# A second MLP product with wide matmuls, a third buffer of weight parts, and a fixed VectorE order

## The chip, the cores and the metric

The kernel runs on one core of a Trainium2 chip. The metric is the device time of one execution in microseconds. Five engines work side by side, each through its own list of instructions in order: TensorE (PE in the profile, with its weight loads as PEld), VectorE (DVE), ScalarE (ACT), GpSimd (POOL) and SyncE (SP), whose queue issues most of the transfers. They wait for one another through semaphores.

## The reference

One transformer-like block on x of 2048 tokens by 512 channels, in float32:

```
h  = x + linear_attention(layernorm(x))            # hedgehog feature map, 32 heads of 16
z  = layernorm(h)                                  # (2048, 512)
u  = gelu(z^T @ w1 + b1)                           # over the token axis: (512, 1792)
y  = u @ w2 + b2                                   # (512, 2048)
out = h + y^T
```

Only the last product, `u @ w2` with its bias and the addition to h, concerns the change. It makes an output of 2048 by 512 from 1792 hidden units. Three quarters of the kernel (attention, second layernorm, first MLP product) come before it and stay as they are.

## The kernel before

Products are made at close to float32 accuracy out of a format that TensorE takes at full pace: each operand is split into a high part (rounded, made by ScalarE as a copy) and a low part (the rest, made by VectorE as a subtraction), and a product is three matmuls: high by high, high by low, low by high. The function `mm3` (lines 61 to 65) does so in the earlier stages, always with 512 columns.

The second MLP product (lines 722 to 859) uses a Winograd-like scheme on blocks of two by two: for two row tiles of the output and two halves of its columns it needs seven block products where a plain product needs eight. The terms used below:

- A *pair* is two output tiles of 128 tokens (`sp`, eight of them). A *step* is one pair `sp` with one pair of hidden tiles `p` (seven of them), so there are 56 steps. A step makes seven block products, each of three matmuls 128 by 128 by 256 (L801): the left operand is one of seven combinations of w2's blocks, the right one of seven combinations of the hidden units' blocks with its high and low part side by side (`UB[p, m]`, 2 by 256 columns).
- A *group* is two steps (`GRP`). `stream_w2` (L779) prepares the seven combinations of w2 for one group: two transfers into `wraw` (L785), four additions and subtractions on VectorE (L789 to L792, here the *block sums*), the high part `whi` on ScalarE and the low part `wlo` on VectorE (the function `split`, L58 and L59; each over 1792 columns). `wraw` has three buffers, `whi` and `wlo` two each. The block sums read and write all of a `wraw`, so ScalarE's copy of that group comes after them.
- The seven products of a pair add up, over its seven steps, in four PSUM banks of 2 by 256 columns. Pairs take the four banks of pool `ps_b` and the four of `ps_f` and `ps_q` in turn. When a pair is done, ScalarE copies one half bank (`e`, L832) and VectorE makes the two output tiles from the banks (L833 to L837, here the *pair sums*: three additions of 256 columns and two fused additions of 512). GpSimd's queue adds each tile to h in memory (L839).
- The last pair works differently: its rows of h are loaded early (`hb`, L844) and the last three steps' products are run bank after bank, so that VectorE can finish the banks while others are still in work.

Around this part the program is ordered by a scheduler that lays out each engine's instructions from modelled times. It may move VectorE's block sums, low parts and pair sums past one another, and matmuls of high parts ahead of those of low parts. In the built program, VectorE's block sums run one group ahead: the list reads low part of group g, block sums of group g+2, low part of group g+1, block sums of group g+3, and so on, with the pair sums put between single block sums of one group.

Of the kernel before, what the change touches and what calls it, by code (L numbers as in the profile page):

```python
# [9 lines left out]
F32 = mybir.dt.float32  # L10
F32R = mybir.dt.float32r
AF = mybir.ActivationFunctionType
ALU = mybir.AluOpType
# [4 lines left out]
P = 128  # L18
S, D, H, DH, F = 2048, 512, 32, 16, 1792
NT = S // P  # L20
# [14 lines left out]
def block_kernel(ctx: ExitStack, tc: tile.TileContext, x, xT, wT, phic, wo, w1, b1, w2, b2,  # L35
                 kvmask, ident_in, out):
    nc = tc.nc
# [9 lines left out]
    b2s = cst.tile([P, NT], F32, name="b2s")  # L47
# [8 lines left out]
    def split(hi, lo, src, lo_engine):  # L56

        nc.scalar.activation(hi, src, AF.Copy)  # L58
        lo_engine.tensor_sub(lo, src, hi)  # L59

    def mm3(o, ah, al, bh, bl, first, last):

        nc.tensor.matmul(o, ah, bh, start=first, stop=False)  # L63
        nc.tensor.matmul(o, ah, bl, start=False, stop=False)  # L64
        nc.tensor.matmul(o, al, bh, start=False, stop=last)  # L65


    aq = ExitStack()
    ps_q = ctx.enter_context(tc.tile_pool(name="ps_q", bufs=2, space=PSUM, side="right"))
# [5 lines left out]
    sums = wqp.tile([P, SUMS, NPR, 2, 2], F32, name="smq")  # L75
# [284 lines left out]
    q = {"mm": 0, "logits": 0, "exp": 0, "sum": 0}  # L360
# [39 lines left out]
    for t in range(3, NT - 1):  # L400
        if t + 2 < NT:
            raw = load_x(t + 2)
# [108 lines left out]
    ps_f = ctx.enter_context(tc.tile_pool(name="ps_f", bufs=2, space=PSUM, reuse_waits="tile"))  # L511
# [83 lines left out]
    w2v = w2.rearrange("(k p) s -> p k s", p=P)  # L595
# [9 lines left out]
    def flush(n=None):  # L605
        if n is None:
            his()
        for _ in range(len(LATER) if n is None else min(n, len(LATER))):
            wl_, raw, wh_ = LATER.pop(0)
            LO.append(nc.vector.tensor_sub(wl_, raw, wh_).ins)  # L610
# [7 lines left out]
        COMING.append((wl_, raw, wh_))  # L618
        return wh_, wl_

    PU, WI, LO = {}, {}, []
    FN, FL = [0] * (NF // 2), [0] * (NF // 2)

    def fill_load(p):
        if FL[p] < NT:
            WI[p, FL[p]] = stream(w1v, FL[p], 2, p * 256, 256)
            FL[p] += 2

    def fill(p, pool=None):

        t = FN[p]
        FN[p] = t + 1
        if FL[p] <= t:
            fill_load(p)
            flush()
        if t == 0:
            PU[p] = [pool.tile([P, D], F32, name="pu", tag="pu") for _ in range(2)]
        a, b = WI[p, t - t % 2]
        for c in range(2):
            mm3(PU[p][c], a[:, t % 2, c * P:(c + 1) * P], b[:, t % 2, c * P:(c + 1) * P],  # L640
                HN[t][:, 0], HN[t][:, 1], t == 0, t == NT - 1)

    def q_half(i):
# [89 lines left out]
    U, UB, far = {}, {}, {}  # L733
# [43 lines left out]
    AW = {}  # L777

    def stream_w2(n):  # L779
        steps = STEPS[n:n + GRP]  # L780
        raw = ws.tile([P, GRP, 7, P], F32, name="wraw", bufs=3)
        wh_ = ws.tile([P, GRP, 7, P], F32R, name="whi")
        wl_ = ws.tile([P, GRP, 7, P], F32R, name="wlo")
        for i, (sp, p) in enumerate(steps):
            nc.sync.dma_start(raw[:, i, 0:4].rearrange("p (k i) s -> p k (i s)", k=2),  # L785
                              w2v[:, 2 * p:2 * p + 2, sp * 2 * P:(sp + 1) * 2 * P])
            AW[sp, p] = wh_[:, i], wl_[:, i]
        with tc.issue_after(LO[-18]):
            nc.vector.tensor_add(raw[:, :, 4], raw[:, :, 0], raw[:, :, 2])  # L789
            nc.vector.tensor_sub(raw[:, :, 0], raw[:, :, 1], raw[:, :, 0])  # L790
            nc.vector.tensor_sub(raw[:, :, 5], raw[:, :, 4], raw[:, :, 1])
            nc.vector.tensor_sub(raw[:, :, 6], raw[:, :, 3], raw[:, :, 5])  # L792
        split(wh_, wl_, raw, nc.vector)


    PROD = ((1, 1, 0, 0, True), (2, 6, 2, 1, True), (3, 3, 3, 1, True), (4, 4, 2, 0, False), (0, 0, 1, 0, True),
            (5, 5, 0, 1, False), (6, 2, 3, 0, False))

    def product(o, a, b, start, stop):
        for i, (x, y) in enumerate(((0, 0), (0, 1), (1, 0))):  # L800
            nc.tensor.matmul(o, a[x], b[:, y], start=start and i == 0, stop=stop and i == 2, skip_group_check=True)  # L801

    def products(sp, ps, order):
        for a, b, bk, half, opens in order:
            for p in ps:
                wh_, wl_ = AW[sp, p]
                product(bank[bk][:, half], (wh_[:, a], wl_[:, a]), UB[p, b], p == 0 and opens, p == NP - 1)

    def flat(a):
        return a.rearrange("p k d -> p (k d)")  # L810

    for n, (sp, p) in enumerate(STEPS):
        t = 2 * sp
        last = t + 2 == NT
        if n % GRP == 0:
            stream_w2(n)
        if p == 0:
            pools = [ps_f, ps_f, ps_q, ps_q] if sp % 2 else [ps_b] * 4
            bank = [pool.tile([P, 2, HD], F32, name="py", tag="pu") for pool in pools]
        if p < NP - 1 - 2 * last:  # L820
            products(sp, [p], PROD)
            continue
        if p < NP - 1:
            continue
        by_bank = sorted(PROD, key=lambda m: m[2:4])
# [3 lines left out]
        if not last:  # L829
            products(sp, [p], by_bank)  # L830
            ot = uo.tile([P, 2, 2, HD], F32, name="ot", bufs=1)
            nc.scalar.activation(e[:, 1], bank[0][:, 0], AF.Copy)  # L832
            nc.vector.tensor_add(u2, bank[0][:, 1], e[:, 1])  # L833
            nc.vector.tensor_add(u3, bank[1][:, 0], u2)
            nc.vector.tensor_add(e[:, 0], bank[2][:, 0], u2)
            for i, add in enumerate((u3.unsqueeze(1).to_broadcast([P, 2, HD]), e)):
                nc.vector.scalar_tensor_tensor(ot[:, i], bank[2 + i], b2s[:, t + i:t + i + 1], add,  # L837
                                               op0=ALU.add, op1=ALU.add)
                nc.gpsimd.dma_start(out[(t + i) * P:(t + i + 1) * P, :], flat(ot[:, i]), accum_op=ALU.add)  # L839
            continue  # L840

        hb = [hp.tile([P, 2, HD], F32, name=f"hb{i}") for i in range(2)]
        for i in range(2):
            nc.sync.dma_start(flat(hb[i]), out[(t + i) * P:(t + i + 1) * P, :])  # L844
            nc.vector.tensor_scalar(hb[i], hb[i], b2s[:, t + i:t + i + 1], None, op0=ALU.add)
        products(sp, [p - 2, p - 1, p], by_bank)
        nc.scalar.activation(e[:, 1], bank[0][:, 0], AF.Copy)
        nc.vector.tensor_add(hb[1][:, 1], bank[0][:, 0], hb[1][:, 1])
        nc.vector.tensor_add(u2, bank[0][:, 1], e[:, 1])
        nc.vector.tensor_add(hb[1][:, 0], u2, hb[1][:, 0])  # L850
        nc.vector.tensor_add(u3, bank[1][:, 0], u2)
        nc.vector.tensor_add(hb[0], hb[0], u3.unsqueeze(1).to_broadcast([P, 2, HD]))
        nc.vector.tensor_add(hb[0][:, 0], bank[2][:, 0], hb[0][:, 0])
        nc.vector.tensor_add(hb[1][:, 0], bank[2][:, 0], hb[1][:, 0])
        nc.vector.tensor_add(hb[0][:, 1], bank[2][:, 1], hb[0][:, 1])
        nc.sync.dma_start(out[t * P:(t + 1) * P, :], flat(hb[0]))
        for k, q in ((0, nc.scalar), (1, nc.sync)):
            nc.vector.tensor_add(hb[1][:, k], bank[3][:, k], hb[1][:, k])
            q.dma_start(out[(t + 1) * P:NT * P, k * HD:(k + 1) * HD], hb[1][:, k])


def _layout(A_x, A_wqkv, A_w_phi, A_wo, B_w1, B_b1, B_w2, B_b2):
# [44 lines left out]
```

## Time and profile before

| | |
|---|---|
| median of 3 runs | 526.39 us (526.26 to 526.75) |
| the profiled execution | 526.04 us, of which the span of the instructions 524.3 us |
| TensorE busy | 517.7 us, 99% of the span |
| VectorE busy | 384.5 us, 73% |
| ScalarE busy | 277.8 us, 53% |
| second MLP product | from 378.6 us on; its last matmul starts at 519.61 us |

The profile's page has a chain of work that ended last, followed back from the end; groups of equal instructions with their busy time, the mean duration of one and what ended the idle time ahead of them; lists of waits; and a timeline in which each line has a start, a duration, the engine, the line of the program, what is written and read (`wlo<-wraw,whi`) and, in brackets, idle time before it with what ended it. The windows give each engine's busy time in a stretch, with a count of instructions. A few per cent of the matmul records are missing from a trace, so counts of matmuls come from the program.

### The profile page before, as it was taken

The numbers are of one execution on the slowest core, as the hardware profiler recorded it, in microseconds if no ns is written. First come the engines' busy times: TensorE is split into PE (matmuls) and PEld (weight loads), VectorE is DVE, ScalarE is ACT, GpSimd is POOL, SyncE is SP. The second block draws the span as 40 slices with busy tenths as digits, with TensorE's granted clock in tenths as the row PEclk, the third lists the DMA queues.
The fourth block names the chain that finished last, engine by engine and source line by source line (L and its number), as shares of the span: only waits on it lengthen the run. The fifth ranks groups of instructions, "written<-read, shape, count | busy, mean of one in ns | idle before, by whom it ended". The sixth has DMA issues, their size and how long they took to land.

```text
span 524.3 us, 10150 instructions
## 1 busy us (share of the span) xinstructions
PE 517.7 (99%) x4000; PEld 446.6 (85%) x4000; DVE 384.5 (73%) x681; ACT 277.8 (53%) x475; POOL 229.4 (44%) x174
## 2 busy tenths in 40 slices
PE   8999999999999999999999999999999999999996
PEld 7888888887877777777788888888899999999996
DVE  6893999986997899697336425726668878888774
ACT  6999853434267877767756433426544333343330
POOL 2579698985989999974224000000001101101110
PEclk9999999999999999999999999999999999999999
DMA  8643210021303333333255432532015556535631
GB/s 304 198 132 121 75 47 22 1 83 60 103 21 101 102 101 108 115 101 123 81 173 154 115 101 81 181 102 80 20 41 122 144 139 154 126 123 133 150 71 50
DMA packets 45487, 55.85 MB, mean 107 GB/s; under 512 B 3968, under 2 KB 33024, under 8 KB 45440
## 3 DMA queue, kind: packets, MB, share of 16 engines
q1 hardware_dynamic: 43136, 51.38, 30.9%
q0 software_dynamic: 2016, 3.67, 5.3%
q8 instruction: 31, 0.51, 0.4%
q10 hardware_dynamic: 288, 0.17, 0.1%
q14 instruction: 16, 0.13, 0.1%
HBM read 46.81 MB, written 8.39 MB: 105 GB/s over the span
## 4 chain that ended last, share of the span: by engine, by line
PE 95%; DVE 3%; ACT 1%; issue 0%; DVEq 0%; ACTq 0%
PE py L801 26%; PE pu L63 13%; PE pu L64 12%; PE pu L65 12%; PE pv L64 3%; PE pv L65 3%; PE po L63 3%; PE pv L63 3%; PE po L65 3%; PE po L64 3%; PE pk_ps L63 2%; PE pk_ps L65 2%; PE pk_ps L64 2%; PE pn L549 2%; PE tr L531 2%; PE kvp L208 2%
## 5 line engine op out<-in xcount | busy, mean ns | idle before, releaser
L839 POOL DMA_DIRECT2D out<-ot x14 | 12.4, 996 | 210.9 <-DVE ot L837 210.9
L801 PE MATMUL py<-uf,whi 128*128 128x256 f32 x560 | 96.2, 283 | 0.0
L58 ACT ACTIVATE whi<-wraw 128x1792 fp32r<-128x1792 f32 x28 | 47.7, 1704 | 77.9 <-PE py L801 73.8
L63 PE MATMUL pu<-hs,whi 128*128 128x512 f32 x224 | 87.7, 394 | 0.0
L64 PE MATMUL pu<-hs,whi 128*128 128x512 f32 x224 | 87.2, 389 | 0.0
L65 PE MATMUL pu<-hs,wlo 128*128 128x512 f32 x224 | 86.7, 389 | 0.0
L801 PEld LDWEIGHTS py<-uf,whi 128*128 128x128 f32 x560 | 83.3, 192 | 0.0
L610 DVE TENSOR_TENSOR wlo<-wraw,whi 128x512 fp32r<-128x512 f32 x56 | 47.3, 847 | 44.7 <-ACT whi L603 44.5
L59 DVE TENSOR_TENSOR wlo<-wraw,whi 128x1792 fp32r<-128x1792 f32 x28 | 56.6, 2022 | 18.6 <-ACT whi L58 18.6
L801 PE MATMUL py<-uf,wlo 128*128 128x256 f32 x280 | 69.9, 283 | 0.0
L603 ACT ACTIVATE whi<-wraw 128x512 fp32r<-128x512 f32 x56 | 34.6, 625 | 45.0 <-PE pu L64 40.8
L63 PEld LDWEIGHTS pu<-hs,whi 128*128 128x128 f32 x224 | 42.0, 188 | 9.1 <-ACT hj L581 0.2
L801 PEld LDWEIGHTS py<-uf,wlo 128*128 128x128 f32 x280 | 49.7, 192 | 0.0
L65 PEld LDWEIGHTS pu<-hs,wlo 128*128 128x128 f32 x224 | 42.0, 188 | 8.9
L64 PEld LDWEIGHTS pu<-hs,whi 128*128 128x128 f32 x224 | 42.1, 188 | 8.5
L443 POOL TENSOR_TENSOR ez<-eq,zB 128x1024 f32<-128x1024 f32 x16 | 38.5, 2408 | 4.4 <-ACT zB L487 4.4
L801 PE MATMUL py<-un,whi 128*128 128x256 f32 x224 | 38.4, 283 | 0.0
L196 POOL TENSOR_TENSOR pk<-pk,sk 128x1024 f32<-128x1024 f32 x16 | 31.0, 1941 | 7.7 <-DVE sk L195 5.4
L467 POOL TENSOR_TENSOR eq<-eq,w 128x1024 f32<-128x1024 f32 x16 | 32.4, 2025 | 3.2 <-DVE w L464 3.2
L801 PEld LDWEIGHTS py<-un,whi 128*128 128x128 f32 x224 | 33.2, 192 | 0.1
L200 POOL TENSOR_TENSOR zacc<-zacc,pk 128x1024 f32<-128x1024 f32 x13 | 31.2, 2404 | 0.5
L172 ACT ACTIVATE pk<-pk,r 128x1024 f32<-128x1024 f32 x16 | 18.4, 1147 | 17.9 <-DVE pk L150 17.7
(172 smaller groups left out, 1174.6 us busy)
## 6 DMA issues: line engine op xcount, KB each, us to landing
wraw<-in_w SPq DMA_DIRECT2D x112, 256.0 KB, 2.9
xraw<-in_xT SPq DMA_DIRECT2D x16, 256.0 KB, 3.1
xh<-in_x SPq DMA_DIRECT2D x16, 256.0 KB, 2.6
h<-in_x SPq DMA_DIRECT2D x16, 256.0 KB, 2.7
out<-h SPq DMA_DIRECT2D x16, 256.0 KB, 2.0
out<-ot POOLq DMA_DIRECT2D x14, 256.0 KB, 4.7
wraw<-in_wT SPq DMA_DIRECT2D x12, 256.0 KB, 5.1
wo<-in_wo SPq DMA_DIRECT2D x4, 256.0 KB, 3.8
```

The costliest lines, as they stand in the source:

```text
L58: nc.scalar.activation(hi, src, AF.Copy)
L59: lo_engine.tensor_sub(lo, src, hi)
L63: nc.tensor.matmul(o, ah, bh, start=first, stop=False)
L64: nc.tensor.matmul(o, ah, bl, start=False, stop=False)
L65: nc.tensor.matmul(o, al, bh, start=False, stop=last)
L196: nc.gpsimd.tensor_mul(heads(PK[t]), heads(PK[t]), sk.unsqueeze(2).to_broadcast([P, 2 * H, DH]))
L200: nc.gpsimd.tensor_add(zacc, zacc, PK[t])
L443: nc.gpsimd.tensor_mul(EZ[t], EQ[t], zB)
L467: nc.gpsimd.tensor_mul(heads(EQ[t]), heads(EQ[t]), W[t].rearrange("p g c h -> p (g c h)").unsqueeze(2).to_broadcast([P, 2 * H, DH]))
L603: nc.scalar.activation(wh_, raw, AF.Copy)
L610: LO.append(nc.vector.tensor_sub(wl_, raw, wh_).ins)
L801: nc.tensor.matmul(o, a[x], b[:, y], start=start and i == 0, stop=stop and i == 2, skip_group_check=True)
```

## The change

All of it lies in the second MLP product.

- Of the seven block products, four (P3, P2, P7, P4) are now `wide`: one matmul of w2's high part with the high and low part of the hidden units in one go (512 columns, a whole bank), and one of the low part with the high part (256 columns) into the first half of the same bank. The three others stay `narrow`, with three matmuls of 256 columns. A wide product fills a bank by itself, of which the two halves must be added later. A pair now takes six banks: four of `ps_b`, the same for every pair, and two (P3 and P2) out of `ps_f` or `ps_q` in turn. In each step but the last of a pair, P3 and P2 come first, then P1, P6, P7, P5, P4; in the last step they come last.
- The pair sums become eleven VectorE instructions of 256 columns each: u2, u3, a low half into u3, e, and a fused addition and a low half for each of the four quarter tiles (the first quarter's low half is inside u3).
- The last pair stays narrow throughout, in six banks, with its h loaded and given the bias early (`last_h`), and its final sums in a written order (`last_sums`).
- The parts `whi` and `wlo` get a third buffer each and `wraw` a fourth, in pool `hp`, which lies where the first product's weights were. `stream_w2` now prepares group n/2 + 2, after the matmuls of step n.
- `in_order` fixes the order on each engine: every instruction passed through it is queued behind the one passed before on that engine. It covers all matmuls of the product, ScalarE's `whi` and `e`, and VectorE's block sums, `wlo` and pair sums. VectorE's list in the built program reads, from group 3 on: block sums of group g, low part of group g, block sums of group g+1, low part of group g+1, with a pair's eleven sums, unbroken, between block sums and a low part.

The core of the diff (the loops of the last pair are left out):

```diff
+    def in_order(*ops):
+        for op in ops:
+            with ExitStack() as st:
+                for ins in QUEUE.values():
+                    st.enter_context(tc.issue_after(ins))
+                ins = op().ins
+            QUEUE[ins.engine] = ins
...
+    def w2_sums(g):
+        raw = hp if g % 4 == 3 else ws
+        raw = RAW[g] = raw.tile([P, GRP, 7, P], F32, name="wraw", bufs=1 if g % 4 == 3 else 3)
...
+            in_order(*sums)
...
+    def w2_parts(g):
+        home = hp if g % 3 == 2 else ws
+        wh_ = home.tile([P, GRP, 7, P], F32R, name="whi")
+        wl_ = home.tile([P, GRP, 7, P], F32R, name="wlo")
...
+            in_order(lambda: nc.scalar.activation(wh_, raw, AF.Copy), lambda: nc.vector.tensor_sub(wl_, raw, wh_))
+
+    AHEAD = 2
+    for g in range(AHEAD):
+        w2_sums(g)
+        w2_parts(g)
+    w2_sums(AHEAD)
+
+    def stream_w2(n):
+        g = n // GRP + AHEAD
+        if n % GRP == 0 and g * GRP < len(STEPS):
+            w2_parts(g)
+            if (g + 1) * GRP < len(STEPS):
+                w2_sums(g + 1)
...
+    def wide(o, p, m, sp):
+        wh_, wl_ = AW[sp, p]
+        in_order(lambda: nc.tensor.matmul(o, wh_[:, m[0]], UB[p, m[1]], start=p == 0, stop=False, skip_group_check=True),
+                 lambda: nc.tensor.matmul(o[:, 0], wl_[:, m[0]], UB[p, m[1]][:, 0], start=False, stop=p == NP - 1,
+                                          skip_group_check=True))
...
+        if not end:
+            wide(b3, p, P3, sp)
+            wide(b2, p, P2, sp)
+        narrow(b16[:, 0], [p], P1, sp, True, True)
+        narrow(b16[:, 1], [p], P6, sp, False, True)
+        wide(b7, p, P7, sp)
+        narrow(b5[:, 0], [p], P5, sp, True, True)
+        wide(b4, p, P4, sp)
+        if not end:
+            return
+        wide(b3, p, P3, sp)
+        wide(b2, p, P2, sp)
...
+        in_order(lambda: nc.scalar.activation(e[:, 1], b16[:, 0], AF.Copy),
+                 lambda: nc.vector.tensor_add(u2, b16[:, 1], e[:, 1]),
+                 lambda: nc.vector.tensor_add(u3, b7[:, 0], u2), low_sum(u3, b7),
+                 lambda: nc.vector.tensor_add(e[:, 0], b5[:, 0], u2), tile_sum(0, 0, b5, u3),
+                 tile_sum(0, 1, b4, u3), low_sum(ot[:, 0, 1], b4),
+                 tile_sum(1, 0, b3, e[:, 0]), low_sum(ot[:, 1, 0], b3),
+                 tile_sum(1, 1, b2, e[:, 1]), low_sum(ot[:, 1, 1], b2))
...
+    for n, (sp, p) in enumerate(STEPS):
+        pair_of_tiles(sp, p)
+        stream_w2(n)
```

More of the change, by code (lines that the diff above doesn't have):

```diff
@@ L64, in mm3 @@
         nc.tensor.matmul(o, ah, bl, start=False, stop=False)
-        nc.tensor.matmul(o, al, bh, start=False, stop=last)
+        return nc.tensor.matmul(o, al, bh, start=False, stop=last).ins
     aq = ExitStack()
@@ L776, in block_kernel @@
     GRP = 2
[L777 to L784, printed above, removed]
+    AW, RAW = {}, {}
+    QUEUE = {}
+    def in_order(*ops):
[5 more added lines that the diff above has]
+            QUEUE[ins.engine] = ins
@@ L793, in stream_w2 @@
[L793 to L807, printed above, removed]
+        sums = (lambda: nc.vector.tensor_add(raw[:, :, 4], raw[:, :, 0], raw[:, :, 2]),
+                lambda: nc.vector.tensor_sub(raw[:, :, 0], raw[:, :, 1], raw[:, :, 0]),
+                lambda: nc.vector.tensor_sub(raw[:, :, 5], raw[:, :, 4], raw[:, :, 1]),
+                lambda: nc.vector.tensor_sub(raw[:, :, 6], raw[:, :, 3], raw[:, :, 5]))
@@ new lines, in w2_sums @@
+        if g < AHEAD:
+            with tc.issue_after(LO[-18]):
+                for op in sums:
+                    op()
+        else:
+            in_order(*sums)
[3 more added lines that the diff above has]
+        wl_ = home.tile([P, GRP, 7, P], F32R, name="wlo")
+        for i, step in enumerate(STEPS[g * GRP:(g + 1) * GRP]):
+            AW[step] = wh_[:, i], wl_[:, i]
+        raw = RAW.pop(g)
+        if g < AHEAD:
+            split(wh_, wl_, raw, nc.vector)
+        else:
+            in_order(lambda: nc.scalar.activation(wh_, raw, AF.Copy), lambda: nc.vector.tensor_sub(wl_, raw, wh_))
@@ L813, in block_kernel, with pair_of_tiles @@
+    def pair_of_tiles(sp, p):
         t = 2 * sp
-        last = t + 2 == NT
-        if n % GRP == 0:
-            stream_w2(n)
         if p == 0:
[L818 to L825, printed above, removed]
+            b3, b2 = [new_bank((ps_f, ps_q)[sp % 2]) for _ in range(2)]
+            BK[:] = [new_bank(ps_b) for _ in range(4)] + [b3, b2]
+        b16, b7, b5, b4, b3, b2 = BK
+        end = p == NP - 1
+        if t + 2 == NT:
+            if p < NP - 3 or end:
+                ps = [p - 2, p - 1, p] if end else [p]
+                places = [(b16[:, 0], P1, True), (b16[:, 1], P6, False), (b7[:, 0], P7, True), (b5[:, 0], P5, True),
+                          (b4[:, 0], P4, True), (b3[:, 0], P3, True), (b2[:, 0], P2, True)]
+                for o, m, opens in places if end else places[5:] + places[:5]:
+                    narrow(o, ps, m, sp, opens, True)
+                if end:
+                    last_sums(t, HB)
+            return
[8 more added lines that the diff above has]
+        if not end:
+            return
+        wide(b3, p, P3, sp)
+        wide(b2, p, P2, sp)
@@ L828, in block_kernel @@
         u3 = uo.tile([P, HD], F32, name="u3")
[L829 to L840, printed above, removed]
```

69 lines of the change are left out of this document (45 added, 24 removed).

## The prediction

> **What bounds the kernel now.** I read the page's busy times and its chain of work that ended last first, then the windows of the second product, then the timeline there.
>
> ```profile
> PE 517.7 (99%) x4000; PEld 446.6 (85%) x4000; DVE 384.5 (73%) x681; ACT 277.8 (53%) x475; POOL 229.4 (44%) x174
> PE 95%; DVE 3%; ACT 1%; issue 0%; DVEq 0%; ACTq 0%
> 378.78 137.53 PE py L801 x1146
> 376.58 0.39 PE L63 MATMUL pu<-hs,whi 128*128 128x512 f32 x1
> ...
> 377.26 0.39 PE L63 MATMUL pu<-hs,whi 128*128 128x512 f32 x1
> ...
> 377.94 0.39 PE L63 MATMUL pu<-hs,whi 128*128 128x512 f32 x1
> ```
>
> TensorE carries the chain, and 1146 matmuls of the second product follow one another without a gap, 137.53/1146 = 0.1200 us each for 256 columns. A matmul of 512 columns takes (377.94 - 376.58)/6 = 0.2267 us: three instructions lie between two starts of L63. So whatever saves matmul time here is worth its full size, as long as the engines that feed TensorE stay ahead. How far ahead they are is in the windows, of which each is about one pair (147 matmuls of 0.1200, 17.64 us):
>
> ```profile
> core 0: us, PE busy (x) PEld busy (x) DVE busy (x) ACT busy (x) POOL busy (x), PEclk, DMA share, GB/s
> 396.30:414.00 17.70, 17.70 (x149) 17.70 (x149) 15.30 (x26) 5.50 (x4) 1.94 (x2) 1.00 0.49 121
> 414.00:431.70 17.70, 17.70 (x150) 17.70 (x149) 13.77 (x22) 7.21 (x5) 1.75 (x2) 1.00 0.60 148
> ```
>
> VectorE is busy 15.30 and 13.77 us of 17.70: it has some three us in hand per pair, no more. What it does with them stands in the timeline of one group and a half (VectorE and ScalarE):
>
> ```profile
> 401.14 2.02 DVE L59 TENSOR_TENSOR wlo<-wraw,whi 128x1792 fp32r<-128x1792 f32 x1
> 403.07 0.42 DVE L789 TENSOR_TENSOR wraw<-wraw 128x256 f32<-128x256 f32 x1
> 403.53 0.42 DVE L790 TENSOR_TENSOR wraw<-wraw 128x256 f32<-128x256 f32 x1
> 403.87 0.42 DVE L791 TENSOR_TENSOR wraw<-wraw 128x256 f32<-128x256 f32 x1
> 404.32 0.43 DVE L792 TENSOR_TENSOR wraw<-wraw 128x256 f32<-128x256 f32 x1
> 405.68 2.03 DVE L59 TENSOR_TENSOR wlo<-wraw,whi 128x1792 fp32r<-128x1792 f32 x1 [0.93 <-ACT whi L58]
> 403.94 1.71 ACT L58 ACTIVATE whi<-wraw 128x1792 fp32r<-128x1792 f32 x1 [3.33 <-PE py L801]
> 408.98 1.71 ACT L58 ACTIVATE whi<-wraw 128x1792 fp32r<-128x1792 f32 x1 [3.33 <-PE py L801]
> ```
>
> ScalarE's `whi` at 403.94 starts while VectorE is still at block sums (403.07 to 404.75). Those sums are therefore of a later group; the `whi` had its own sums long before and waited only for TensorE to give back a buffer. That head start of one group is what the changed order does not have.
>
> **The change, part by part.**
>
> *Wide products.* Two matmuls of 256 columns (0.2400) become one of 512 (0.2267), 0.0133 us less, in 4 products x 7 steps x 7 pairs = 196 places: -2.6 us. The rows bound it: at no fixed cost per matmul it would be nothing, at the rows' 0.0133 it is 2.6; the 512-column row is the same form, so I take it. The Trainium skill (TensorE: Matmul & The Clock Gate, "Wait — 56ns, not 53.3ns?") gives a fixed cost of about 2.5 ns for a warm matmul, by which the saving would be an estimated 0.5 us. A step now takes 4 x (0.2267 + 0.1200) + 9 x 0.1200 = 2.467 us, a group 4.93, a pair 17.27.
>
> *Block sums and parts in a fixed order.* VectorE now does, for each group: block sums, then the low part, which needs `whi`, which needs these very sums. Nothing of VectorE's may pass in between, so it stands still while ScalarE copies. The handovers:
>
> ```profile
> 379.54 0.42 DVE L746 TENSOR_TENSOR u<-u 128x256 f32<-128x256 f32 x1 [0.26 <-ACT u L738]
> 380.00 1.03 ACT L58 ACTIVATE uf<-u 128x256 fp32r<-128x256 f32 x3 [0.19 <-DVE u L746]
> DVE wlo L59 <- ACT whi L58: 18.6, 16, 3.0
> ACT whi L58 <- PE py L801: 73.8, 25, 3.3
> ```
>
> From VectorE's end to ScalarE's start 380.00 - 379.96 = 0.04; from the start of `whi` to the start of its `wlo` 405.68 - 403.94 = 1.74. From one `wlo` start to the next it is then 1.93 (403.07 - 401.14) + 1.68 for the block sums to their end (404.75 - 403.07) + 0.04 + 1.74 = 5.39 us. TensorE uses up a group in 4.93. VectorE and ScalarE, in turn, become slower than TensorE. The two rows of waits show today's case: ScalarE waits for TensorE (73.8 us), VectorE for ScalarE only 18.6 in all; I expect the first to shrink and the second to double.
>
> *Pair sums.* Eleven instructions of 256 columns in place of three of 256 and two of 512. Their pace:
>
> ```profile
> 516.75 0.42 DVE L848 TENSOR_TENSOR hb<-py,hb 128x256 f32<-128x256 f32 x1 [3.20 <-ACT e L847]
> 517.09 0.41 DVE L849 TENSOR_TENSOR u<-py,e 128x256 f32<-128x256 f32 x1
> 517.54 0.42 DVE L850 TENSOR_TENSOR hb<-u,hb 128x256 f32<-128x256 f32 x1
> 399.82 0.74 DVE L837 SCALAR_TENSOR_TENSOR ot<-py,b2s,u 128x512 f32<-128x512 f32 x1
> 400.48 0.74 DVE L837 SCALAR_TENSOR_TENSOR ot<-py,b2s,e 128x512 f32<-128x512 f32 x1
> ```
>
> An instruction follows an unrelated one after 0.34 us, and one whose result it reads after 0.45. Five of the eleven read the one before (u3, its low half, three low halves): 5 x 0.45 + 6 x 0.34 = 4.3 us (ends: 3.7 with all at 0.34, 5.0 with all at 0.45). A fused addition of 256 columns is not in this trace; half of 0.66 (400.48 - 399.82) says 0.33, so 0.34 holds. During the pair sums ScalarE can copy the next `whi`, so a group with pair sums in it takes 1.93 + 1.59 (block sums, 1.25 to the last start and 0.34 on) + 4.3 = 7.8 us.
>
> *The sum of VectorE's loop.* A pair is three and a half groups, so two pairs are seven: five plain ones and two with pair sums, 5 x 5.39 + 2 x 7.8 = 42.6 us. TensorE's share is 2 x 17.27 = 34.5. The loop closes because a pair's banks in `ps_b` are the next pair's: TensorE cannot start P1 of the next pair until u2 has read its bank, and u2 stands in VectorE's list behind all earlier groups' work. So every two pairs 8.1 us are lost. Between the sums of the first and of the seventh pair lie three times two pairs: +24.2 us. Laying the instructions of a pair end to end gives the shape: at the end of the second, fourth and sixth pair, which have four groups between their sums and the last, u2 comes about 5.9 us after the pair's last matmul and TensorE waits some 6.7 us (5.8 for P1's bank, 1 more for P7's, P5's and P4's); at the third, fifth and seventh it is about 0.5 us late and TensorE waits 1.4.
>
> At the start, two groups are ready and the chain begins when `hp` is given back at the last matmul of the first product; I lay out a wait of 1.0 us after the first pair (0 to 3: a transfer late by its usual three us would move it). At the end the last `wlo`, behind the seventh pair's sums, comes 0.8 us late. Together 24.2 + 1.0 + 0.8 = 26.0 us.
>
> Bounds of the loop: 15 plain groups with a ScalarE handover between 0 and 0.08 us on both sides (-1.2 to +1.2 together) and six pair sums at 3.7 to 5.0 us (-3.6 to +4.2), so 21 to 31.
>
> *The third buffer.* It lets `whi` start a group sooner, and today's ScalarE waits are for that buffer. But `whi` now waits for the sums ahead of it: 0 us.
>
> *The last pair.* The order puts P1's and P6's banks first, so the final sums start earlier.
>
> ```profile
> 519.61 0.28 PE L801 MATMUL py<-uf,wlo 128*128 128x256 f32 x1
> 520.13 0.75 DVE L858 TENSOR_TENSOR hb<-py,hb 128x256 f32<-128x256 f32 x2
> ```
>
> Today the last matmul ends at 519.89 and the last sum at 520.88, since eight sums are still in line. The eight take 3.4 us (516.75 to 520.13) and will have 45 matmuls, 5.4 us, so only the last sum (0.04 + 0.42) is left: 520.35, -0.5 us.
>
> *Other moves.* The two loads of h for the last pair move on SP's queue ahead of the weights of group 3, and VectorE's two bias additions with them: 0 us, as four `wraw` buffers stand ahead of need; were they late, it is the three us at the start named above. GpSimd's fourteen transfers stay the same in number. PSUM's `ps_f` and `ps_q` banks come back after two pairs. Restarting TensorE costs about 0.1 us, from a row of another stage:
>
> ```profile
> 147.35 0.68 DVE L558 TENSOR_TENSOR ol<-pn,oh 128x512 fp32r<-128x512 f32 x1
> 148.09 0.50 PE L63 MATMUL po<-woh,oh 128*128 128x512 f32 x1
> 148.42 0.39 PE L64 MATMUL po<-wol,oh 128*128 128x512 f32 x1
> ```
>
> The first matmul after a wait is followed after 0.33 us, not 0.2267. While VectorE sets the pace this is hidden in its loop.
>
> **Sum.** 526.04 - 2.6 + 26.0 - 0.5 = 548.9 us for the profiled execution. Its 526.04 lies 0.35 below the median of the runs, so on their scale 549.3 us. A measurement here tells 0.2%, some 1 us, from no change.
>
> **Rivals.**
>
> *It is faster, 523.3 us (526.39 - 3.1).* This is so if VectorE's wait for `whi` doesn't add up: the busy times alone (seven groups at 1.93 + 1.59 and two pair sums of 4.3, 33.2 us for two pairs) fit into TensorE's 34.5. It decides at the exposed wait: five times 1.87 us per two pairs must fall to a quarter of a us each. Against it: `whi` reads all seven combinations in one instruction, so it can't start on part of them. Chance 5%.
>
> *The sums run ahead as before and only the pair's end costs: 527.2 us.* Then `whi` of a second, fourth or sixth pair's last group is freed by TensorE two steps (4.93 us) before the pair's end, and 0.1 + 1.74 + 1.93 + 1.59 later u2 starts, 0.4 us late; the chain down to P4's bank makes it 1.3 us of waiting, three times, +3.9 - 3.1. Chance 3%.
>
> *TensorE slows down after its long waits: up to 551.7 us.* The first matmuls of the program, after idleness, go at half pace:
>
> ```profile
> 1.06 4.21 PE pk_ps L289 x18
> 7.71 1.80 PE pv L269 x16
> 2.00:3.00 1.00, 1.00 (x7) 1.00 (x6) 0.00 (x0) 0.47 (x1) 0.00 (x0) 1.00 0.74 251
> PE pk_ps L289 <- DVE eps L54: 1.1, 1, 1.1
> ```
>
> That is 234 ns each for 128 columns at first and 112 later, for some 4.2 us, though the window's granted clock reads 1.00. After each of the three waits of 5.8 us it would cost 2.1 us; but VectorE paces, and the next pair's 1.4 us of waiting and its slack take that up. Only a slow stretch of 6.8 us or more shows, as +2.4 us. The longest wait of TensorE in this trace is 1.1 us, so it has no case of it. The Trainium skill (TensorE: Matmul & The Clock Gate, "Why this matters for your kernels") has idle gaps over about 3 us bring the array back to half its clock. Chance that it shows in the time: 15%.
>
> *The loop costs more, about 560 us:* each handover 0.08 us dearer and pair sums at 5 us, or transfers late at each group. Chance 7%.
>
> **How the numbers follow.** The likeliest, 70%, is VectorE's loop with the sum above, 549.3, own range 544 to 554. With the slow clock inside and the loop's bounds, 542 to 556 holds about 8 in 10; the faster case, the small case and the dearest one are left out. Slower by over 0.2%: 0.92 (70 + 15 + 7); within: 0.03; faster: 0.05.
>
> **What would show it.** The matmul line of the wide products at about 0.227 us apart. VectorE's `wlo` waiting for ScalarE's `whi` about 1.8 us in most groups, and `whi` waiting for VectorE's block sums and hardly for TensorE. TensorE's idle time put down to VectorE's pair sums, with three waits of 5 to 6 us and the others small; its share of the span near 94%. The last sum under 0.6 us after the last matmul. The prediction is wrong if TensorE has no gaps at the pairs' ends, if block sums are seen between `whi`'s start and its `wlo`, or if the gaps are alike at all pairs.

## The result, and the profile after

The changed kernel takes 554.63 us (median of five runs, 554.23 to 554.76); the kernel before took 526.39 us (median of five, 525.69 to 526.75). The ratio is 1.0536, with a 95% interval of 1.0520 to 1.0551: slower, and 5.3 us above the 549.3 us of the prediction, inside its range of 542 to 556 and just over the 544 to 554 that it gave its likeliest case. The profiled execution took 554.63 us too, with a span of 552.9 us where it was 524.3.

The page of the changed kernel: busy times, the chain that ended last, and, of the slices, TensorE's busy tenths and its granted clock.

```profile
PE 525.8 (95%) x3804; PEld 441.7 (80%) x3804; DVE 399.1 (72%) x723; ACT 277.2 (50%) x475; POOL 228.8 (41%) x174
PE   8999999999999999999999999999895995995997
PEclk9999999999999999999999999999997997998899
PE 68%; DVE 17%; issue 7%; ACT 6%; DMA 1%; SPq 0%; ACTq 0%; DVEq 0%
```

TensorE's row shows a hole in three slices (the 5s), at the ends of the second, fourth and sixth pair, and a smaller one beside the first pair. A quarter of the chain has gone from TensorE (95% to 68%) to VectorE (3% to 17%), ScalarE (1% to 6%) and `issue` (0% to 7%), the time in which an engine waited for nothing that the profile shows. The clock row dips (7s and 8s) in the same places; an experiment below tells what that is worth.

The waits of the second product (us in total, times, longest):

```profile
ACT whi L816 <- DVE wraw L798: 91.2, 21, 6.5
DVE wlo L816 <- ACT whi L816: 32.4, 17, 2.2
PE py L839 <- DVE u L898: 19.4, 5, 5.8
```

Read against the two rows of before in the prediction: ScalarE's copy `whi` no longer waits for TensorE but for VectorE's last block sum (L798), and VectorE's wait for `whi` has gone from 18.6 to 32.4 us. TensorE waits for `u2` (L898), the sum that frees its bank at a pair's end, with a longest wait of 5.8 us.

VectorE's list from the first pair's sums to the end of the two groups behind them:

```profile
398.22 0.41 DVE L898 TENSOR_TENSOR u<-py,e 128x256 f32<-128x256 f32 x1
...
402.48 0.42 DVE L894 TENSOR_TENSOR ot<-py,ot 128x256 f32<-128x256 f32 x1
402.82 2.02 DVE L816 TENSOR_TENSOR wlo<-wraw,whi 128x1792 fp32r<-128x1792 f32 x1
404.75 0.42 DVE L795 TENSOR_TENSOR wraw<-wraw 128x256 f32<-128x256 f32 x1
...
406.00 0.43 DVE L798 TENSOR_TENSOR wraw<-wraw 128x256 f32<-128x256 f32 x1
408.32 2.02 DVE L816 TENSOR_TENSOR wlo<-wraw,whi 128x1792 fp32r<-128x1792 f32 x1 [1.89 <-ACT whi L816]
413.83 2.03 DVE L816 TENSOR_TENSOR wlo<-wraw,whi 128x1792 fp32r<-128x1792 f32 x1 [1.89 <-ACT whi L816]
```

and ScalarE's copy of the same stretch, with TensorE's first matmul after the hole at the second pair's end:

```profile
406.58 1.70 ACT L816 ACTIVATE whi<-wraw 128x1792 fp32r<-128x1792 f32 x1 [6.48 <-DVE wraw L798]
423.33 0.79 PE L839 MATMUL py<-un,whi 128*128 128x256 f32 x2 [5.84 <-DVE u L898]
```

The loop can be read off the starts: the last block sum ends at 406.43, `whi` starts at 406.58, `wlo` at 408.32, the next `wlo` at 413.83. In each plain group (one without pair sums) VectorE stands still for 1.89 us while ScalarE copies, and ScalarE stands still while VectorE makes the low part and the next block sums. One such group takes 413.83 - 408.32 = 5.51 us, and TensorE uses one up in 4.93.

### The profile page after: what moved, and what is told of

It reads as the page before. It is cut to its first block, busy times and chain, and to the rows that moved or that the text cites. A ratio compares the mean times of both kernels' runs of the same rounds, so it can differ in the third digit from the quotient of the medians.

```text
span 552.9 us, 9799 instructions
## 1 busy us (share of the span) xinstructions
PE 525.8 (95%) x3804; PEld 441.7 (80%) x3804; DVE 399.1 (72%) x723; ACT 277.2 (50%) x475; POOL 228.8 (41%) x174
## 4 chain that ended last, share of the span: by engine, by line
PE 68%; DVE 17%; issue 7%; ACT 6%; DMA 1%; SPq 0%; ACTq 0%; DVEq 0%
PE pu L63 12%; PE pu L64 12%; PE pu L65 11%; ACT whi L816 5%; DVE wlo L816 3%; PE pv L64 3%; PE pv L65 3%; PE po L63 3%; PE py L839 3%; PE pv L63 3%; PE po L65 2%; PE po L64 2%; PE pk_ps L63 2%; PE pk_ps L64 2%; PE pk_ps L65 2%
## 5 line engine op out<-in xcount | busy, mean ns | idle before, releaser
L816 ACT ACTIVATE whi<-wraw 128x1792 fp32r<-128x1792 f32 x26 | 44.2, 1702 | 105.8 <-DVE wraw L798 91.2
L816 DVE TENSOR_TENSOR wlo<-wraw,whi 128x1792 fp32r<-128x1792 f32 x26 | 52.6, 2022 | 34.2 <-ACT whi L816 32.4
L839 PE MATMUL py<-uf,whi 128*128 128x256 f32 x280 | 53.3, 282 | 0.0
L845 PE MATMUL py<-uf,whi 128*128 128x512 f32 x140 | 52.6, 396 | 0.0
L839 PEld LDWEIGHTS py<-uf,whi 128*128 128x128 f32 x280 | 43.2, 189 | 3.0
L839 PE MATMUL py<-un,whi 128*128 128x256 f32 x112 | 25.4, 320 | 20.0 <-DVE u L898 19.4
L839 PE MATMUL py<-uf,wlo 128*128 128x256 f32 x140 | 39.8, 284 | 0.3 <-DVE wlo L816 0.3
L846 PE MATMUL py<-uf,wlo 128*128 128x256 f32 x140 | 39.2, 280 | 0.0
L839 PEld LDWEIGHTS py<-un,whi 128*128 128x128 f32 x112 | 19.6, 215 | 24.0 <-DVE u L898 21.0
L467 POOL TENSOR_TENSOR eq<-eq,w 128x1024 f32<-128x1024 f32 x16 | 32.4, 2023 | 3.2 <-DVE w L464 3.2
```

The costliest lines, as they stand in the source:

```text
L467: nc.gpsimd.tensor_mul(heads(EQ[t]), heads(EQ[t]), W[t].rearrange("p g c h -> p (g c h)").unsqueeze(2).to_broadcast([P, 2 * H, DH]))
L816: in_order(lambda: nc.scalar.activation(wh_, raw, AF.Copy), lambda: nc.vector.tensor_sub(wl_, raw, wh_))
L839: in_order(lambda: nc.tensor.matmul(o, x[:, m[0]], UB[p, m[1]][:, y], start=opens and p == 0 and i == 0, stop=closes and p == NP - 1 and i ...
L845: in_order(lambda: nc.tensor.matmul(o, wh_[:, m[0]], UB[p, m[1]], start=p == 0, stop=False, skip_group_check=True), lambda: nc.tensor.matm ...
L846: lambda: nc.tensor.matmul(o[:, 0], wl_[:, m[0]], UB[p, m[1]][:, 0], start=False, stop=p == NP - 1, skip_group_check=True))
```

## The experiments

Theory A is the prediction's: block sums directly ahead of the copy that needs them tie VectorE and ScalarE into one loop, which is slower than TensorE. Theory B: the cost comes from something else in the change, that is from TensorE itself (wide products, the slow clock after long waits) or from the written order as such.

**The block sums one group ahead.** The changed kernel; only the place of the block sums in the order is changed: those of group g+2 are written behind the parts of group g, not those of g+1.

```diff
+    w2_sums(AHEAD + 1)
...
-            if (g + 1) * GRP < len(STEPS):
-                w2_sums(g + 1)
+            if (g + 2) * GRP < len(STEPS):
+                w2_sums(g + 2)
```

> Edit to the changed kernel: VectorE's block sums run one group further ahead (sums of group g+2 after the low part of group g); nothing else. Theory A (VectorE stands still in every group while ScalarE makes the high part, because the sums that it needs come right before): the 1.9 us waits of the low parts for the high parts go, two pairs take TensorE's 34.5 us and some waits of 1.3 to 1.5 us after the second, fourth and sixth pair; with about 4 us lost at the start, 530 to 532 us. Rival B (the eleven unbroken pair sums before the next pair's banks are the cost, not the wait for the high part): the long waits stay, above 545 us. Rival C (TensorE's slow clock after long waits is a large part): about 548 us or more as long as long waits stay.

Measured: 528.22 us (528.07 to 528.76), 1.0045 of the kernel before (1.003 to 1.006), which took 525.85 us in these runs. 26 of the 28 us are gone. VectorE's list now (the first two `wlo` behind the first pair's sums), and the seven `u2` with their first and last start:

```profile
399.91 2.02 DVE L816 TENSOR_TENSOR wlo<-wraw,whi 128x1792 fp32r<-128x1792 f32 x1
403.43 2.02 DVE L816 TENSOR_TENSOR wlo<-wraw,whi 128x1792 fp32r<-128x1792 f32 x1
```

```profile
L899 DVE TENSOR_TENSOR u<-py,e x7: 416/419/425, 395.3 to 503.8; 128x256 f32<-128x256 f32 x7
```

A group takes 3.52 us in place of 5.51, with no stop for `whi`. TensorE's hole of 5.8 us is gone. From the first to the seventh `u2` it is 503.8 - 395.3 = 108.5 us, where six pairs are 103.6 of TensorE: some 4.9 us are still lost, chiefly at the ends of the second, fourth and sixth pair, where the block sums stand between the last `wlo` and `u2`. This is the prediction's third case made as a kernel ("the sums run ahead and only the pair's end costs"), which it had put at 527.2 us.

**The block sums behind the pair's sums.** The same kernel, and at those three pairs the block sums are written behind the pair's sums.

```diff
-    AW, RAW = {}, {}
+    AW, RAW, LATE = {}, {}, []
...
             if (g + 2) * GRP < len(STEPS):
-                w2_sums(g + 2)
+                if (n + 2) % NP == 0:
+                    LATE.append(g + 2)
+                else:
+                    w2_sums(g + 2)
+        elif LATE:
+            w2_sums(LATE.pop())
```

> As the run before, and the block sums that stand right ahead of the second, fourth and sixth pair's sums are put behind them. Theory A: these pairs' first sum now starts 1 us before the pair's end, the three waits of 1.3 to 1.5 us go, 526 to 528 us with the start's 4 us still lost. Rival B: no change against the run before, since the eleven sums stay in one piece.

Measured: 523.84 us (523.50 to 524.43), 0.9963 of the kernel before (0.9949 to 0.9977). Run once more:

> The kernel of e2_sums_after_pair once more, unchanged, on one chip with the kernel before, for an interval on its gain and against e5_two_for_wide (0.9991 of the kernel before). Wide products worth 2.6 us: ratio 0.994 to 0.995. Worth 1.5 us: 0.996.

Measured: 523.95 us (523.83 to 523.96), 0.9964 (0.9951 to 0.9976). It beats both kernels, with every part of the change in it and another order. The expectations of the two kernels (530 to 532 and 526 to 528) were too high. The short waits at the three pairs' ends were worth 4.4 us (528.22 - 523.84), about what had been expected. What did not come is the loss of about 4 us at the start that both expectations had left in: the first `u2` starts at 395.3 with the sums ahead, and at 398.2 in the changed kernel. The `u2` of the kernel with the sums behind the pair's sums, and TensorE's first and last matmul of the second product:

```profile
L904 DVE TENSOR_TENSOR u<-py,e x7: 415/419/425, 395.3 to 499.2; 128x256 f32<-128x256 f32 x7
378.24 0.39 PE L851 MATMUL py<-un,whi 128*128 128x512 f32 x1
...
517.82 0.28 PE L845 MATMUL py<-uf,wlo 128*128 128x256 f32 x1
```

From the first to the last start it is 139.58 us, against 140.99 before (378.62 to 519.61): 1.4 of the 2.6 us of the wide products arrive. Where the rest stays was not followed; six pairs take 499.2 - 395.3 = 103.9 us, 0.3 more than 103.6, so most of it lies outside them. With the 0.5 us forecast for the earlier last sums this fits the measured gain of 1.9 us (525.80 - 523.95).

**The wide products, taken apart in both kernels.** In each wide product the matmul of 512 columns is made as two of 256 again, once in the changed kernel and once in the kernel just told of.

```diff
-        in_order(lambda: nc.tensor.matmul(o, wh_[:, m[0]], UB[p, m[1]], ...),
+        in_order(lambda: nc.tensor.matmul(o[:, 0], wh_[:, m[0]], UB[p, m[1]][:, 0], ...),
+                 lambda: nc.tensor.matmul(o[:, 1], wh_[:, m[0]], UB[p, m[1]][:, 1], ...),
```

> The changed kernel with each wide product taken apart again into two matmuls of 256 columns; the fixed order and the buffers stay. Theory A (VectorE's loop sets the pace): TensorE's 2.6 us more are taken out of its own waits; only the first pair and the last one are paced by TensorE, so 554.6 to 555.2 us, at most +0.6. Theory B (the wide products are worth their 2.6 us wherever they stand): 557.2 us.

> The kernel of e2_sums_after_pair (block sums a group ahead, TensorE nearly without waits, 523.8 us) with each wide product as two matmuls of 256 columns. Theory A: here TensorE is the bound and 196 x 0.0133 us return in full, 526.4 us. Rival (a fixed cost of 2.5 ns per matmul, 196 x 0.0025): 524.3 us.

Measured: in the changed kernel 554.68 us (ratio 1.0541, 1.0526 to 1.0555), no different from 554.63. In the kernel with the sums ahead 525.65 us (0.9991, 0.9982 to 1.0000), 1.7 us more than the 523.95, or 1.4 us by the two ratios, since the two were measured on different chips. It lies between the 526.4 us of theory A and the 524.3 of the rival, nearer to theory A. The pages' busy times, the wide kernel first and the one with them taken apart second:

```profile
PE 515.5 (99%) x3804; PEld 435.5 (83%) x3804; DVE 397.9 (76%) x723; ACT 277.0 (53%) x475; POOL 228.7 (44%) x174
```

```profile
PE 518.3 (99%) x4000; PEld 447.0 (85%) x4000; DVE 398.5 (76%) x723; ACT 277.1 (53%) x475; POOL 228.8 (44%) x174
```

196 matmuls more make 2.8 us of TensorE's time. Where TensorE is the bound, 1.4 to 1.7 of that shows in the end; where VectorE paces, nothing does. So the saving is real and the changed kernel cannot collect it. The fixed cost of about 2.5 ns for a warm matmul that the Trainium skill gives (TensorE: Matmul & The Clock Gate, "Wait — 56ns, not 53.3ns?") would have made it an estimated 524.3 us. The measurement is above that. The pitch of a wide product in the trace of the changed kernel (two starts of L845 at 395.60 and 395.95, 0.35 us) agrees with the prediction's 0.2267 + 0.1200:

```profile
395.60 0.40 PE L845 MATMUL py<-uf,whi 128*128 128x512 f32 x1
395.83 0.28 PE L846 MATMUL py<-uf,wlo 128*128 128x256 f32 x1
395.95 0.39 PE L845 MATMUL py<-uf,whi 128*128 128x512 f32 x1
```

**A longer copy, in both kernels.** ScalarE's high part is made by seven copies of 256 columns in place of one of 1792.

```diff
-            in_order(lambda: nc.scalar.activation(wh_, raw, AF.Copy), lambda: nc.vector.tensor_sub(wl_, raw, wh_))
+            in_order(*[lambda m=m: nc.scalar.activation(wh_[:, :, m], raw[:, :, m], AF.Copy) for m in (6, 0, 1, 2, 3, 4, 5)],
+                     lambda: nc.vector.tensor_sub(wl_, raw, wh_))
```

> The changed kernel with ScalarE's high part as seven copies of 256 columns in place of one of 1792, the one that needs the last block sum first, so that all seven stand behind the sums. About 0.31 us from one to the next and 0.41 for the last make 2.24 us for 1.70: 0.54 us more in each group whose high part VectorE waits for, 15 of them, so +8 us. Theory A (the copy stands in VectorE's loop): 562 to 563 us. Theory B (ScalarE, half idle, is off the path): 554.6 us.

> The kernel of e2_sums_after_pair, in which VectorE hardly waits for ScalarE's high part since the block sums run a group ahead, with that high part as seven copies of 256 columns (the same edit that was worth +9 us in the changed kernel). Theory A (a copy costs only where it stands in VectorE's loop): 523.5 to 525 us. Theory B (seven copies cost by themselves, through ScalarE's queue or the waits that they bring): 530 us or more.

Measured: 563.75 us (563.55 to 564.21; ratio 1.0717, 1.0702 to 1.0731) in the changed kernel, +9.1; 525.65 us (525.37 to 526.08; 0.9995, 0.9986 to 1.0004) with the sums ahead, +1.7. VectorE in the changed kernel with seven copies:

```profile
409.78 2.03 DVE L817 TENSOR_TENSOR wlo<-wraw,whi 128x1792 fp32r<-128x1792 f32 x1 [2.41 <-ACT whi L816]
415.81 2.02 DVE L817 TENSOR_TENSOR wlo<-wraw,whi 128x1792 fp32r<-128x1792 f32 x1 [2.41 <-ACT whi L816]
```

The wait grows from 1.89 to 2.41 us and the group from 5.51 to 6.03, by about what the copy is longer, and the time lies just over theory A's band (562 to 563); ScalarE is busy half of the span either way. The control is dearer than expected (523.5 to 525), and its waits say where: the copy is still awaited three times, in the group ahead of the sums of the second, fourth and sixth pair. First the row of the changed kernel with seven copies, then the control's:

```profile
DVE wlo L817 <- ACT whi L816: 41.1, 18, 2.4
```

```profile
DVE wlo L817 <- ACT whi L816: 2.0, 3, 0.7
```

Against the 32.4 us of the changed kernel the first is 8.7 more, for 9.1 in the time; the second's 2.0 us stand for 1.7. So the control agrees with theory A's rule: the copy costs about what VectorE waits for it.

**TensorE kept busy in its long waits.** 46 matmuls into an unused half bank, which nothing reads, stand behind the second, fourth and sixth pair. This is added work; the rest is the changed kernel.

```diff
+        if sp % 2 == 1:
+            wh_, _ = AW[sp, p]
+            for _ in range(46):
+                in_order(lambda: nc.tensor.matmul(b5[:, 1], wh_[:, 0], UB[p, 0][:, 0], start=False, stop=True, ...))
```

> The changed kernel with 46 extra matmuls of 256 columns (5.5 us) after the second, fourth and sixth pair, into an unused half bank, so that TensorE is busy where it waited 5.8 us. Theory A: VectorE sets the pace, so the slow clock after those waits was paid for by it anyway; granted clock 1.00 throughout, and the time 554.6 us within 1.0. Rival C: three stretches of 6 us at about 0.57 of the pace are gone, 2.6 us each, 547 to 549 us.

Measured: 554.38 us (554.05 to 554.86; 1.0542, 1.0526 to 1.0557): no different. The windows of the wait, of the six microseconds behind it and of the next ones, in the changed kernel (busy times by engine, then the granted clock, DMA share and GB/s):

```profile
417.00:423.00 6.00, 0.49 (x4) 0.17 (x2) 4.02 (x7) 1.97 (x2) 0.00 (x0) 0.95 0.33 111
423.30:429.20 5.90, 5.87 (x23) 5.48 (x24) 5.68 (x11) 1.50 (x1) 1.72 (x2) 0.50 0.44 92
429.30:435.00 5.70, 5.70 (x42) 5.29 (x41) 3.74 (x7) 1.70 (x1) 0.00 (x0) 1.00 0.67 142
```

and in the kernel with the added matmuls:

```profile
423.30:429.20 5.90, 5.51 (x35) 4.51 (x34) 5.76 (x12) 1.09 (x1) 1.72 (x2) 1.00 0.51 85
```

After its first long wait TensorE does run at a granted clock of 0.50 for 5.9 us, with 23 matmuls recorded where 42 come in 5.7 us at full clock. The Trainium skill (TensorE: Matmul & The Clock Gate, "Why this matters for your kernels") has idle gaps of over about 3 us bring the array back to half its clock, and the trace agrees: the wait was 5.84 us. Behind the second and third long wait the slow stretch is shorter, 3.1 and 3.4 us; here is the second, from the restart on:

```profile
467.15:470.20 3.05, 3.05 (x12) 2.95 (x13) 2.93 (x8) 1.44 (x1) 0.28 (x1) 0.50 0.24 82
```

With the clock kept up the time stays. What became of the loss is seen at the third pair's end, in ScalarE's `e`, which needs TensorE's results, and VectorE's `u2` behind it, first in the changed kernel, then with the added matmuls:

```profile
441.19 0.39 ACT L897 ACTIVATE e<-py 128x256 f32<-128x256 f32 x1 [2.75 <-PE py L839]
442.00 0.42 DVE L898 TENSOR_TENSOR u<-py,e 128x256 f32<-128x256 f32 x1
```

```profile
439.24 0.39 ACT L902 ACTIVATE e<-py 128x256 f32<-128x256 f32 x1 [1.22 <-PE py L839]
441.59 0.42 DVE L903 TENSOR_TENSOR u<-py,e 128x256 f32<-128x256 f32 x1
```

`e` is done 1.96 us before `u2` starts when the clock is kept up, and still 0.42 us before it when it is not. What TensorE lost at half clock was time that VectorE's list left it.

**No written order.** All parts of the change, with the order left to the scheduler (which places instructions by modelled times).

```diff
-            with ExitStack() as st:
-                for ins in QUEUE.values():
-                    st.enter_context(tc.issue_after(ins))
-                ins = op().ins
-            QUEUE[ins.engine] = ins
+            op()
```

> The changed kernel with wide products, third buffers and eleven pair sums, but with no fixed order: the scheduler places VectorE's, ScalarE's and TensorE's instructions. In its list the block sums stand one to three groups ahead of their low parts. Theory A: no exposed wait for the high part in most groups, 523 to 530 us. Rival B (more and longer pair sums cost by themselves): 535 us or more.

Measured: 531.89 us (531.57 to 532.59; 1.0115, 1.010 to 1.013), a little over the expected band. The loop is gone here too, so some 23 us of the slowdown belong to this written order. Among what is left are TensorE's waits for the weights' parts:

```profile
PEld py L842 <- DVE wlo L812: 2.6, 7, 0.7
PEld py L841 <- ACT whi L812: 2.5, 6, 0.6
```

A written order is therefore not the fault by itself: the one with the sums ahead and behind the pair's sums is 8 us better than the scheduler's. Why the scheduler's `whi` comes late was not followed further.

**Two buffers of parts in place of three**, once with the sums ahead and once in the changed kernel. The parts are then written one step later, when the buffer of two groups before is free.

```diff
-        home = hp if g % 3 == 2 else ws
+        home = ws
...
-        if n % GRP == 0 and g * GRP < len(STEPS):
+        if n % GRP == 1 and g * GRP < len(STEPS):
```

> The kernel of e2_sums_after_pair with two buffers of high and low parts in place of three (the parts of a group are then written one step later, when the buffer of two groups before is given back). Theory A: one step (2.5 us) is then all that lies between a buffer's return and its next use, where high and low part take 1.7 + 2.0 = 3.7 us; TensorE waits at most groups for the parts: over 530 us, up to 20 x 1.5 = 30 us more. Rival (the third buffer is worth nothing once the sums run ahead, as the prediction took it): 523.8 us.

> The changed kernel itself with two buffers of high and low parts in place of three (the parts of a group, and the next group's block sums, then stand one step later in the order). The prediction put the third buffer at 0 us because the high part waits for the block sums anyway. Theory A (VectorE's loop of 5.5 us a group paces, TensorE gives a buffer back in 4.93): 552 to 560 us. Theory C (the third buffer is worth in this order what it was worth with the sums ahead, 540.2 - 523.9): about 571 us.

Measured: 540.23 us (540.04 to 540.28; 1.0268, 1.0254 to 1.0282) with the sums ahead, 16.3 more than with three buffers; 561.0 us (560.89 to 561.59; 1.0667, 1.0649 to 1.0685) in the changed kernel, 6.4 more. The first is as theory A had it; the second lies just over A's band and ten below theory C. With the sums ahead, ScalarE's wait for TensorE to give a buffer back grows; the row with three buffers first, with two second:

```profile
ACT whi L816 <- PE py L851: 29.5, 11, 3.3
```

```profile
ACT whi L816 <- PE py L851: 49.2, 13, 5.4
```

The changed kernel with two buffers, around the first pair's sums:

```profile
395.90 2.02 DVE L816 TENSOR_TENSOR wlo<-wraw,whi 128x1792 fp32r<-128x1792 f32 x1 [1.85 <-ACT whi L816]
403.42 1.70 ACT L816 ACTIVATE whi<-wraw 128x1792 fp32r<-128x1792 f32 x1 [7.28 <-PE py L845]
405.16 2.02 DVE L816 TENSOR_TENSOR wlo<-wraw,whi 128x1792 fp32r<-128x1792 f32 x1 [1.04 <-ACT whi L816]
```

With two buffers the copy of this group does not run beside the pair's sums, since TensorE hands its buffer back only at 403.42; `wlo` then waits 1.04 us behind the sums, and the group takes 9.26 us (405.16 - 395.90) in place of 8.13. The groups with the third, fifth and seventh pair's sums take 9.2 us too, those with the second, fourth and sixth pair's stay at 8.1; four times 1.1 us are most of the 6.4. The later place in the order is part of these two figures: with two buffers, parts made at the old place would overwrite weights that the next step still reads. What the buffer alone is worth is not shown.

## Why the prediction was right, and where its sizes were off

The forecast's case came true, 5.3 us dearer than its sum. On the spans the change cost 552.9 - 524.3 = 28.6 us, where the sum said 22.9. Term by term:

| term of the sum | predicted us | measured us |
|---|---|---|
| VectorE's loop, `u2` of the first to `u2` of the seventh pair, beyond TensorE's 6 x 17.27 | +24.2 | +28.0 |
| first pair and last `wlo` | +1.8 | +3.7 |
| wide products | -2.6 | -2.6 in TensorE's pace |
| last pair's sums | -0.5 | -0.5 |

The measured loop is from one row of the changed kernel, the seven `u2` with their first and last start: 529.8 - 398.2 = 131.6, less the 103.6 of six pairs of TensorE.

```profile
L898 DVE TENSOR_TENSOR u<-py,e x7: 415/416/418, 398.2 to 529.8; 128x256 f32<-128x256 f32 x7
```

The second line is what is left of TensorE's loss. Its matmuls take 7 x 17.27 + 17.64 = 138.5 us; from the first start to the end of the last (these two rows, and VectorE's last sum)

```profile
378.87 0.39 PE L845 MATMUL py<-un,whi 128*128 128x512 f32 x1
548.96 0.28 PE L839 MATMUL py<-uf,wlo 128*128 128x256 f32 x1
549.27 0.42 DVE L932 TENSOR_TENSOR u<-py,u 128x256 f32<-128x256 f32 x1 [0.65 <-PE py L839]
```

it is 170.2 (548.96 + 0.12 - 378.87), so 31.7 us were lost, 28.0 of them in the loop and 3.7 outside it.

*The loop* is the mechanism, and the experiments show it: with the sums ahead its cost is gone, with the copy longer it grows by 0.52 us a group, with TensorE's work longer or its clock up it stays. Two prices in it were too low. A plain group takes 5.51, not 5.39 us, nearly all of it the handover from VectorE to ScalarE: 0.15 us (406.43 to 406.58) where the prediction took 0.04 from one row of another form; fifteen groups make 1.7. The eleven pair sums take 402.82 - 398.22 = 4.60 us, not 4.3, about half of it because an instruction that reads the result of a fused addition starts 0.51 us after it, where 0.45 was taken; so a group with pair sums takes 8.13, not 7.8 us (394.69 to 402.82, from `wlo` to `wlo`), and six of them make 2.0. The pair sums lay inside their bounds (3.7 to 5.0), the handover beyond its upper end of 0.08. Both misses go the same way, so nothing cancelled by luck.

*The first pair* was put at 1.0 us with 0 to 3 as bounds. Its `e` was done at 395.12, but `u2` started 3.1 us later, at 398.22, because a low part and four block sums stood ahead of it in VectorE's list, and TensorE waited 1.54 us for it. Rows of ScalarE, VectorE and TensorE (the bracket of `wlo` names TensorE, but ScalarE's copy that it reads ended at 394.65, just ahead of it):

```profile
394.73 0.39 ACT L897 ACTIVATE e<-py 128x256 f32<-128x256 f32 x1
```

```profile
387.00 0.42 DVE L798 TENSOR_TENSOR wraw<-wraw 128x256 f32<-128x256 f32 x1
...
394.69 2.03 DVE L816 TENSOR_TENSOR wlo<-wraw,whi 128x1792 fp32r<-128x1792 f32 x1 [1.83 <-PE py L839]
```

```profile
398.69 0.51 PE L839 MATMUL py<-un,whi 128*128 128x256 f32 x2 [1.54 <-DVE u L898]
```

The loop starts later than laid out, since its first block sums were threaded between VectorE's last splits of the hidden units and ended only at 387.42. How the 3.7 us divide between the first pair and the last `wlo` was not worked out.

*The shape* came nearly as laid out: three waits of 5.8 us at the second, fourth and sixth pair and one of 1.5 at the first, TensorE's share 95% for the 94% forecast, `whi` waiting for block sums, `wlo` for `whi` by 1.89 us (forecast 1.8), the last sum 0.45 us behind the last matmul (549.24 to 549.69; 0.99 before). VectorE's wait for `whi` grew from 18.6 to 32.4 us, short of the doubling expected. The 1.4 us forecast for the third, fifth and seventh pair did not come: TensorE's five waits for `u2`, 19.4 us in all, are the three long ones, the 1.54 us at the first pair and 0.43 us at the fifth. In the kernel with the added matmuls, where the clock stayed up, there are seven such waits, one at each pair's end, 0.40 us at the third; so the slow clock had used up the time in which TensorE would have waited.

*The wide products* were counted as -2.6 us on top of a loop that was worked out against the shorter TensorE time, and so cancel inside it. The prediction called a saving "worth its full size, as long as the engines that feed TensorE stay ahead"; here they do not stay ahead, and taken apart again the wide products change nothing (554.68).

*The third buffer at 0 us* is the step with the weakest reason. That `whi` waits for the sums anyway holds for plain groups; in the group with the first pair's sums the copy runs beside the sums only because a buffer is free, and every second group with pair sums grows as much without it. With two buffers and the parts a step later 6.4 us were added, and 16.3 where the sums run ahead; what the buffer alone is worth stays open.

*The rivals.* The slow clock came about (0.50, for 5.9 us the longest time) but did not show in the time, as the main forecast had it: the next pair's slack took it up, with 0.4 us to spare at the third pair. That the sums run ahead and only the pair's end costs was not this kernel's case; built on purpose it gave 528.2 for a forecast of 527.2. The faster case needed the wait for `whi` to fall to a quarter; written that way, the kernel gives 523.9 for a forecast of 523.3.

## What to carry to other kernels

When an order is written by hand, look for an instruction whose result another engine turns round for the next instruction of the same list: both engines then work in turn, and their busy shares (here 72% and 50%) say nothing of it. Put the producer one round ahead of its consumer, and put work that frees a bank ahead of work that only prepares. Cost such a loop by starts read from the trace, handovers included, and compare it with what the bound engine needs per round before asking what the other parts of a change are worth.

## What the runs showed of the hardware

After three waits of 5.8 us TensorE ran at a granted clock of 0.50, for 5.9 us after the first and for 3.1 and 3.4 us after the others, and a kernel that filled the waits with 46 matmuls each kept 1.00. The handover from VectorE to ScalarE took 0.15 us behind the block sums where another pair of instructions showed 0.04. A fused addition of 256 columns out of PSUM let an instruction that reads its result start after 0.51 us, and another fused one after 0.40.
